# One chip core, three chained layers: coarse attention computed once per pair of units instead of once per unit

## The chip, the cores and the metric

The kernel runs on one core of a Trainium2 chip. The metric is device time in microseconds of one execution of the whole program. Three runs of the kernel before gave 643.84, 644.37 and 645.01 us (median 644.37).

## The reference

Three layers follow each other. The change touches the coarse half of the first.

```python
# first layer: B=4, H=8, S=576, D=64, factor=4, Sd=144
q_d = q.reshape(B, H, Sd, factor, D).mean(axis=3)      # k_d, v_d likewise
out_d = sm_attn(q_d, k_d, v_d)                         # softmax(q_d k_d^T / 8) v_d
out_up = np.repeat(out_d, factor, axis=2)
...
scores = np.where(|i - j| < factor, scale * q k^T, -1e9)
out_local = softmax(scores) v
attn_out = out_up + out_local
# second layer: token mixing, then channel mixing
u = x + (relu(x^T w_tok1) w_tok2)^T
x2 = u + relu(u w_ch1) w_ch2
# third layer: four causal attention experts, the two best of a gate mixed
```

## The kernel before, in words

A **unit** is one batch and one pair of heads: 16 units, numbered `4*b + p`. Head 0 of a unit lies on partitions 0 to 63, head 1 on 64 to 127. A **pair** `k` is units `2k` and `2k+1`. The first stage of the program is the attention of all units and the token mixing of each pair (`half`), woven together; the channel mixing (tiles `c`, line 219) and the third layer follow.

The order of every instruction of the first stage is written out by hand in the table `STEPS`: each word is a step and its unit, pair or part, and the words are issued from left to right, each engine taking its own instructions in that order. An instruction that waits holds everything behind it on its engine. Steps of a unit that matter here: `q` and `v` load; `qd`, `kd`, `pv` add up groups of four; `sl` is the local scores (band and product, TensorE), `mx`, `ex`, `sm`, `rs`, `P` their softmax, `tl` and `tc` turn and copy the result. The coarse attention of a unit is `sd` (scores, TensorE), `md` (maximum, VectorE), `ed` (Exp with its sum, ScalarE), `rd` (reciprocal of the sum, VectorE), `Pd` (scaling, GpSimd), `pdt` (six transposes) and `pc` (copy out of PSUM, tile `PdT`). Steps of a pair: `ol` is the product with the values for both units (coarse and local), `oc` and `ad` copy and add it into `u`. Steps of the token mixing of a pair: `tx` (turn `u`), `xh`, `xl` (split in two parts; `xr` is the rest of 64 rows), `h` (first product), `hh`, `hl`, `pu` (second product), `ua` (add into `u`). Words such as `w0`, `g0`, `t0`, `a0`, `f0`, `gd0`, `add0`, `hi0`, `lo0` load and convert the weights.

In the coarse scores of a unit the 144 pooled queries lie in two blocks of 72 (`c`) and the result stands on 72 partitions; `h` selects the half of the array's rows and the PSUM bank:

```python
for c in range(2):
    for h in range(2):
        mm(sd[:72, h, c * SD:(c + 1) * SD], qd[64 * h:64 * h + 64, c * 72:(c + 1) * 72],
           kd[64 * h:64 * h + 64, :], start=True, stop=True)
```

PSUM has four single banks (`b1`: `tl`, `pdt`, `ol`, `tx`, `h`, `pu`) and two double banks (`b2`) in this stage; `sl` and `sd` take the double ones in turn.

Of the kernel before, what the change touches and what calls it, by code (L numbers as in the profile page):

```python
# [7 lines left out]
F32 = mybir.dt.float32  # L8
# [4 lines left out]
AF = mybir.ActivationFunctionType  # L13
OP = mybir.AluOpType
# [14 lines left out]
PB = 3  # L29
# [22 lines left out]
    q0 sl0 q1 qd0 mx0 kd0 kd1 w0 g0 t0 w1 qd1 sd1 sb0 gd0 a0 ex0 sl1 f0 q2 g1 md1 sm0 mx1 ed1 gd1 rd1 q3 a1 rs0 add0  # L52
    sl2 hi0 ex1 qd2 kd2 w2 f1 t1 mx2 sd0 sb2 lo0 g2 sl3 Pd1 pdt1 md0 q4 qd4 gd2 rs1 v0 a2 P0 t2 kd3 ex2 add1 ed0 kd4
    mx3 P1 pc1 w3 rd0 sl4 f2 hi1 Pd0 ex3 tl0.0 tl0.1 sm2 tc0.0 add2 v1 tl1.0 pdt0 q5 lo1 pv0 w4 hi2 pv1 g3 tl1.1 mx4
    sd2 qd3 sb4 rs2 lo2 pc0 tc1.0 ex4 rs3 sd3 gd3 q6 md2 tc1.1 a3 tc0.1 P3 md3 t3 g4 ed2 gd4 ol0.0 a4 ol0.1 f3 f4
    kd5 oc0 ed3 sd4 ad0.0 add3 t4 ad0.3 ad0.2 ad0.1 tl3.0 md4 P2 tx0.1 rd3 hi3 add4 lo3 tc3.0 xh0.1 tx0.0 tx0.2
    tl3.1 xh0.0 v2 q7 xh0.2 ed4 Pd3 xl0.1 xl0.0 sl5 xl0.2 pdt3 pv2 tl2.0 sl6 rd2 sm4 hi4 tc3.1 w5 Pd2 kd6 mx5 tc2.0
    g5 qd5 t5 h0.0 gd5 tl2.1 rs4 v3 a5 f5 ex5 q8 h0.1 w6 lo4 mx6 sd5 pc3 tc2.1 qd6 hh0 pdt2 add5 P4 sb6 hi5 tl4.0 g6
    pc2 sd6 tc4.0 hl0 pv3 ol1.0 md5 ol1.1 t6 ed5 sl7 q9 lo5 gd6 v4 rd4 a6 md6 f6 oc1 add6 ed6 kd7 ad1.0 ad1.2 ad1.1
    pu0.0 ad1.3 mx7 tl4.1 tx1.0 rs5 tx1.1 hi6 tc4.1 xh1.0 lo6 ua0.0 v5 sl8 xh1.1 P5 rd6 Pd4 pu0.1 pu0.2 ex7 xl1.0 w7  # L60
    ua0.1 q10 pv4 xl1.1 qd7 kd9 q11 tx1.2 ua0.2 xh1.2 xl1.2 pdt4 qd9 tl5.0 rd5 sd7 pv5 h1.0 Pd5 kd10 w8 qd8 md7 ex6
    pc4 g7 Pd6 pu0.3 h1.1 mx8 sb8 kd8 sl9 v6 ed7 hh1 ua0.3 q12 sm6 tc5.0 v7 rs7 hl1 pdt5 mx9 rd7 g8 gd8 rs6 pc5
    tl5.1 pu1.0 P6 tc5.1 ua1.0 ex9 gd7 sd8 ol2.0 md8 P7 pu1.1 Pd7 oc2 ex8 ed8 pv6 ua1.1 v8 q13 sd9 pu1.2 rs9 ad2.0
# [82 lines left out]
def body(ctx, tc, qT, kT, vw, vp, wt1, wt2, wc1, wc2, wq, wk, wvg, wo, out):  # L146
# [193 lines left out]
    NR = pa.tile([72, 6], F32, name="ndraw")  # L340
    SR = [pa.tile([72, 6], F32, name=f"sdm{i}") for i in range(3)]
    for x in (NR, *SR):
        nc.gpsimd.memset(x, 1.0)

    turns = {"pd": 0, "vr": 0, "sr": 0}

    def rotate(nm, tiles):
        turns[nm] += 1
        return tiles[(turns[nm] - 1) % len(tiles)]

    def unit(i):
# [16 lines left out]
        def pool_q():  # L368
            r["qd"] = pa.tile([128, SD], F32, tag="qd", bufs=4, name="qd")
            nc.vector.tensor_reduce(r["qd"], r["q"].rearrange("p (g r) -> p g r", r=4), axis=AX.X, op=OP.add)  # L370
# [69 lines left out]
        def down():  # L440
            sd, qd, kd = b2("sd"), r["qd"], r["kd"]
            for c in range(2):
                for h in range(2):
                    mm(sd[:72, h, c * SD:(c + 1) * SD], qd[64 * h:64 * h + 64, c * 72:(c + 1) * 72],  # L444
                                     kd[64 * h:64 * h + 64, :], start=True, stop=True)
            r["sd"] = sd[:72, :, :2 * SD].rearrange("p h (c k) -> p h c k", c=2)

        def down_max():
            nd = r["nd"] = pa.tile([72, 3, 3], F32, tag="nd", bufs=3, name="nd")
            nc.vector.tensor_reduce(NR[:, :4].rearrange("p (h c) -> p h c", h=2), r["sd"], axis=AX.X, op=OP.max, negate=True)  # L450
            nc.vector.tensor_scalar_mul(nd[:, :, :2], NR.rearrange("p (h c) -> p h c", c=2), 1.0 / 128.0)

        def down_exp():
            Pd = r["Pd"] = rotate("pd", PD)
            sdm = r["sr"] = rotate("sr", SR)
            for h in range(2):
                for c in range(2):
                    nc.scalar.activation(Pd[:, :, c, h, :KD], r["sd"][:, h, c].rearrange("p (j k) -> p j k", k=KD), AF.Exp, bias=r["nd"][:, h, c:c + 1],
                                         scale=1.0 / 128.0, accum_out=sdm[:, 2 * c + h:2 * c + h + 1])

        def down_sum():
            rd = pa.tile([72, 3, 3], F32, tag="rd", bufs=3, name="rd")
            nc.vector.tensor_scalar(rd[:, :, :2], r["sr"].rearrange("p (c h) -> p c h", h=2), 1e-9, 4.0, op0=OP.add, op1=OP.mult)
            r["rd"] = pa.tile([72, 4], F32, tag="rd4", bufs=3, name="rd4")
            nc.vector.reciprocal(r["rd"].rearrange("p (c h) -> p c h", h=2), rd[:, :2, :2])

        def down_norm():
            P4 = r["Pd"].rearrange("p j c h n -> p j (c h) n")[:, :, :, :KD]
            nc.gpsimd.tensor_tensor(P4, P4, r["rd"][:, None, :, None].to_broadcast([72, 3, 4, KD]), op=OP.mult)

        def turn_down():
            pd = r["pdt"] = b1("pdt")
            for j in range(3):
                for c in range(2):
                    o = j * SD + c * 72
                    tp(pd[:, o:o + 72], r["Pd"][:, j, c].rearrange("p h n -> p (h n)"), ident[:72, :72])

        def keep_down():
            r["PdT"] = pa.tile([128, 3, SD], F32, tag="PdT", bufs=4, name="PdT")
            nc.scalar.activation(r["PdT"].rearrange("p j n -> p (j n)"), r["pdt"][:, :3 * SD], AF.Copy)  # L480
# [583 lines left out]
```

## Time and profile before

| | before |
|---|---|
| median of three runs | 644.37 us |
| profiled execution | 644.59 us, of which span 642.5 us |
| TensorE (PE) busy | 618.0 us, 96% |
| VectorE (DVE) busy | 443.6 us, 69% |
| ScalarE (ACT) busy | 361.5 us, 56% |
| GpSimd (POOL) busy | 149.5 us, 23% |

The span runs from the first to the last instruction that the profiler saw; 2.1 us of the execution lie around it. Busy shares are means over the span: the first 48 us, the rest of the first stage, the channel mixing and the third layer differ. TensorE's matmuls overlap each other, so the duration of one is longer than the distance to the next; distances are what add up.

### The profile page before, as it was taken

Reading aid. Unit: us, or ns where it says so; the run is one execution under the profiler, and the core shown is the slowest. Engines: PE = TensorE matmul, PEld = TensorE weight load, DVE = VectorE, ACT = ScalarE, POOL = GpSimd, SP = SyncE. Lnnn points to the kernel's source line nnn. Section 1 sums busy time; section 2 is a strip of 40 time slices with the busy share of each in tenths; the row PEclk is TensorE's granted clock in tenths of the full one; section 3 lists DMA queues with packets and bytes.
Section 4 is the critical chain, followed back from the end, with each engine's and each line's share of the span. In section 5 each row is a group of like instructions: output and inputs, shape, how many; then the busy total and the mean of one; then the engine's idle time right before and its main releaser. Section 6 shows DMA issues by size and latency. Waiting matters only on the chain.

```text
span 642.5 us, 13638 instructions
## 1 busy us (share of the span) xinstructions
PE 618.0 (96%) x5196; PEld 554.6 (86%) x5196; DVE 443.6 (69%) x1083; ACT 361.5 (56%) x1061; POOL 149.5 (23%) x167
## 2 busy tenths in 40 slices
PE   4789999999999999999999999999989999999997
PEld 3678889999988889998888889999989889989885
DVE  7999998779696876467644554443497766857871
ACT  4898977765464453343422332420488777777783
POOL 6878986522131120010000000310010020010000
PEclk9999999999999999999999999999999999999999
DMA  8879484013132220020200100000111121021103
GB/s 266 250 234 279 130 248 119 13 46 116 42 106 88 66 87 12 1 66 0 67 0 1 51 16 1 2 0 1 44 35 37 29 76 38 20 100 40 37 33 117
DMA packets 28945, 46.76 MB, mean 73 GB/s; under 512 B 3216, under 2 KB 16016, under 8 KB 28880
## 3 DMA queue, kind: packets, MB, share of 16 engines
q1 hardware_dynamic: 28880, 45.90, 23.8%
q8 instruction: 41, 0.67, 0.5%
q14 instruction: 24, 0.20, 0.1%
HBM read 36.45 MB, written 4.72 MB: 64 GB/s over the span
## 4 chain that ended last, share of the span: by engine, by line
PE 87%; DVE 9%; DMA 1%; issue 1%; ACT 1%; POOL 1%; SPq 0%; ACTq 0%; DVEq 0%; POOLq 0%
PE c L219 47%; PE proj L219 7%; PE vp L219 4%; PE wo L219 4%; PE pu L219 4%; PE o L962 4%; PE pt L939 3%; PE h L219 3%; PE s L900 2%; PE s L901 2%; DMA wt_raw<-in_wt_dram 1%; PE tx L556 1%; PE sd L444 1%; DVE nraw L403 1%; PE tl L486 1%
## 5 line engine op out<-in xcount | busy, mean ns | idle before, releaser
L219 PE MATMUL c<-hl,wch 128*128 128x460 f32 (+1 forms) x240 | 89.3, 372 | 0.0
L219 PE MATMUL c<-hh,wcl 128*128 128x460 f32 (+1 forms) x240 | 89.1, 371 | 0.0
L219 PE MATMUL c<-hh,wch 128*128 128x460 f32 (+1 forms) x240 | 89.1, 371 | 0.0
L219 PE MATMUL c<-ul,wch 128*128 128x460 f32 (+1 forms) x240 | 89.0, 371 | 0.0
L219 PE MATMUL c<-uh,wch 128*128 128x460 f32 (+1 forms) x240 | 89.0, 371 | 0.0
L219 PE MATMUL c<-uh,wcl 128*128 128x460 f32 (+1 forms) x240 | 88.9, 370 | 0.0
L199 ACT ACTIVATE hh<-c 128x460 fp32r<-128x460 f32 (+1 forms) x60 | 33.0, 549 | 84.9 <-PE c L219 84.6
L795 POOL TENSOR_TENSOR vlo<-u,vh 128x576 fp32r<-128x576 f32 x16 | 22.8, 1427 | 238.7 <-ACT vh L791 215.1
L208 DVE SCALAR_TENSOR_TENSOR hl<-c,hh 128x460 fp32r<-128x460 f32 (+1 forms) x60 | 38.0, 634 | 48.7 <-ACT hh L199 48.5
L281 POOL TENSOR_TENSOR wc_t<-wc_f,wc_t 128x512 int32<-128x512 int32 x24 | 32.5, 1358 | 150.7 <-ACT wc_t L270 122.3
L663 DVE TENSOR_TENSOR ul<-u,uh 128x460 fp32r<-128x460 f32 (+1 forms) x80 | 53.1, 677 | 9.7 <-ACT uh L657 9.7
L657 ACT ACTIVATE uh<-u 128x460 fp32r<-128x460 f32 (+1 forms) x80 | 45.4, 585 | 23.8 <-PE c L219 19.0
L917 ACT ACTIVATE Pc<-Pc,nm 116x116 f32<-116x116 f32 (+4 forms) x80 | 46.7, 586 | 8.7 <-DVE nm L910 6.8
L910 DVE CUSTOM_DVE_ANT_0 Pc<-s,caus 116x348 f32<-116x348 f32 (+4 forms) x80 | 40.0, 514 | 14.6 <-PE s L901 10.9
L219 PEld LDWEIGHTS c<-hh,wch 128*128 128x128 f32 x240 | 45.2, 188 | 5.2
L219 PEld LDWEIGHTS c<-hh,wcl 128*128 128x128 f32 x240 | 45.1, 188 | 5.2
L219 PEld LDWEIGHTS c<-uh,wcl 128*128 128x128 f32 x240 | 45.1, 188 | 5.1
L219 PEld LDWEIGHTS c<-uh,wch 128*128 128x128 f32 x240 | 45.1, 188 | 5.0
L219 PEld LDWEIGHTS c<-hl,wch 128*128 128x128 f32 x240 | 45.1, 188 | 4.9
L219 PEld LDWEIGHTS c<-ul,wch 128*128 128x128 f32 x240 | 45.1, 188 | 4.9
L939 PE MATMUL pt<-ident,Pc 116*116 116x116 f32 (+2 forms) x240 | 35.2, 263 | 2.9 <-DVE Pc L928 2.6
L928 DVE TENSOR_SCALAR Pc<-Pc,su,gw 116x464 f32<-116x464 f32 (+4 forms) x80 | 36.3, 478 | 0.7
(216 smaller groups left out, 1650.6 us busy)
## 6 DMA issues: line engine op xcount, KB each, us to landing
wc_raw<-in_wc_dram SPq DMA_DIRECT2D x24, 512.0 KB, 3.6
vz<-in_vw_dram SPq DMA_DIRECT2D x16, 320.0 KB, 5.3
qT<-in_qT_dram SPq DMA_DIRECT2D x16, 288.0 KB, 5.0
kT<-in_kT_dram SPq DMA_DIRECT2D x16, 288.0 KB, 5.3
vr<-in_vp_dram SPq DMA_DIRECT2D x32, 144.0 KB, 4.2
K<-K SPq DMA_DIRECT2D x64, 72.0 KB, 2.0
out_dram<-y SPq DMA_DIRECT2D x18, 256.0 KB, 2.0
wt_raw<-in_wt_dram SPq DMA_DIRECT2D x4, 288.0 KB, 3.5
```

Source lines behind the costliest of these rows:

```text
L199: nc.scalar.activation(hi, src, AF.Relu if relu else AF.Copy, **({"scale": scale} if scale else {}))
L208: nc.vector.scalar_tensor_tensor(lo, src, 0.0, h, op0=OP.max, op1=OP.subtract)
L219: mm(ps, a, c, start=first and i == 0, stop=last and i == n - 1)
L281: nc.gpsimd.tensor_tensor(t, r["f"], t, op=OP.add)
L657: nc.scalar.activation(hi, UA[:, c, blocks[k]], AF.Copy)
L663: nc.vector.tensor_tensor(lo, UA[:, c, blocks[k]], hi.bitcast(F32), op=OP.subtract)
L795: nc.gpsimd.tensor_tensor(lo, U[b][:, c], hi.bitcast(F32), op=OP.subtract)
L910: nc.vector.tensor_tensor_reduce(dst, r["s", t, e], mask, -1.0, 3.0e38, OP.add, OP.min, nm[:nq])
L917: nc.scalar.activation(P[:nq, :n], P[:nq, :n], AF.Exp, bias=r["nm", t, e][:nq], scale=-1.0, accum_out=r["su", t][:nq, e:e + 1])
L928: nc.vector.tensor_scalar(P[:nq, :n], P[:nq, :n], r["su", t][:nq, e:e + 1], BR[b]["w"][:nq, t, 2 * p + e:2 * p + e + 1], op0=OP.mult, op1= ...
L939: tp(pt[:TS[c], (c - c0) * TQ:(c - c0) * TQ + nq], P[:nq, c * TQ:c * TQ + TS[c]], ident[:nq, :nq])
L962: mm(o[64 * e:64 * e + 64, a - q0:q1 - q0], BR[b]["VV"][:TS[c], c, ec:ec + 64], PT[e][:TS[c], column(c, a):column(c, a) + q1 - a], start=( ...
```

## The change

The coarse attention becomes a step of a pair. The 288 pooled queries of two units are cut into six blocks of 48; set `s` holds blocks `2s` and `2s+1`, one on partitions 0 to 63, one on 64 to 127. A block is issued 64 queries wide (the last 16 are the next block's, or zeros that a memset writes once), so that each score matmul uses one quarter of the array: 12 matmuls of 64 x 64 with 144 columns for a pair, where two units had 8 of 64 x 72. Maximum, Exp, reciprocal and scaling then act on 128 partitions and three sets for both units at once: one maximum over 864 numbers a partition for two over 576, six Exp for eight, one scaling over 864 for two over 576. Each (j, s) block of 112 rows is turned with a permutation `perm` in place of the identity, which drops the 16 surplus queries behind the 96 useful ones, where the next block overwrites them: nine transposes of 112 columns for twelve of 72, again in two single banks, and two copies for two. The buffers `pd` are two (of 128 partitions) instead of three; the memsets of `ndraw` and `sdm` go, memsets of `qd` and three copies that build `perm` come. The whole table `STEPS` is another one.

```diff
-PB = 3
+PB = 2
+ROWS = 64 + KD
 STEPS = """
-    q0 sl0 q1 qd0 mx0 kd0 kd1 w0 g0 t0 w1 qd1 sd1 sb0 gd0 a0 ex0 sl1 f0 q2 g1 md1 sm0 mx1 ed1 gd1 rd1 q3 a1 rs0 add0
...
+    q0 sl0 qd0 q1 mx0 sl1 sb0 qd1 ex0 w0 kd0 kd1 mx1 sm0 g0 ex1 q2 t0 rs0 kd2 gd0 w1 P0 g1 sd0 a0 f0 sl2 md0 add0
...
-    PD = [pa.tile([72, 3, 2, 2, 64], F32, name=f"pd{i}") for i in range(PB)]
+    PD = [pa.tile([128, 3, 3, 2, 64], F32, name=f"pd{i}") for i in range(PB)]
+    perm = pa.tile([ROWS, ROWS], F32, name="perm")
+    for to, at, n in ((0, 0, KD), (KD, 64, KD), (2 * KD, KD, 64 - KD)):
+        nc.vector.tensor_copy(perm[:, to:to + n], ident[:ROWS, at:at + n])
+    QD = [pa.tile([128, SD + 16], F32, name=f"qd{i}") for i in range(4)]
...
+        def down():
+            sd = b2("sd")
+            for s in range(3):
+                for c in range(2):
+                    x, t = divmod(2 * s + c, 3)
+                    for h in range(2):
+                        hs = slice(64 * h, 64 * h + 64)
+                        mm(sd[64 * c:64 * c + 64, h, s * SD:(s + 1) * SD], (A, Bu)[x]["qd"][hs, KD * t:KD * t + 64],
+                           (A, Bu)[x]["kd"][hs], start=True, stop=True)
+            r["sd"] = sd[:, :, :3 * SD].rearrange("p h (s k) -> p h s k", s=3)
...
+        def down_max():
...
+            nc.vector.tensor_reduce(raw.rearrange("p (s h) -> p h s", h=2), r["sd"], axis=AX.X, op=OP.max, negate=True)
+            nc.vector.tensor_scalar_mul(nd[:, :, :2], raw.rearrange("p (s h) -> p s h", h=2), 1.0 / 128.0)
...
+            for s, h in SH:
+                nc.scalar.activation(Pd[:, :, s, h, :KD], r["sd"][:, h, s].rearrange("p (j k) -> p j k", k=KD), AF.Exp,
+                                     bias=r["nd"][:, s, h:h + 1], scale=1.0 / 128.0, accum_out=sm[:, 2 * s + h:2 * s + h + 1])
...
+        blocks_d = [(j, s) for j in range(3) for s in range(3)]
+
+        def turn_down(part):
+            pd = r["pdt", part] = b1("pdt")
+            for n, (j, s) in enumerate(blocks_d[5 * part:5 * part + 5]):
+                tp(pd[:, 2 * KD * n:2 * KD * n + ROWS], r["Pd"][:ROWS, j, s].rearrange("p h n -> p (h n)"), perm)
...
+            n0, n1 = (0, 10 * KD, 18 * KD)[part:part + 2]
+            nc.scalar.activation(r["PdT"][:, n0:n1], r["pdt", part][:, :n1 - n0], AF.Copy)
```

How the new table moves instructions is seen in two places. The first is the start of VectorE's queue, from the first pooling `qd` to the first weight conversions (`nraw` are local maxima, `P` the local scores shifted, `sm` and `rs` their sums and reciprocals, `nd` and `ndraw` the coarse maxima, `rd` the coarse reciprocals, `wt_0_g`, `wt_0_a`, `wt_0_f` the conversion of the first weight). Before:

```order
L370 TENSOR_REDUCE qd<-qT_0_137 128x144
L403 TENSOR_REDUCE nraw<-sl 128x2x5
L370 TENSOR_REDUCE qd<-qT_1_166 128x144
L412 TENSOR_TENSOR P_0_199<-sl,nraw 128x2x5x64
L278 TENSOR_SCALAR wt_0_g<-wt_0_g 128x512
L272 TENSOR_SCALAR wt_0_a<-wt_0_g 128x512
L275 SCALAR_TENSOR_TENSOR wt_0_f<-wt_0_raw,wt_0_a 128x512
L450 TENSOR_REDUCE ndraw<-sd 72x4
```

And in the change:

```order
L371 TENSOR_REDUCE qd_111<-qT_0_139 128x144
L404 TENSOR_REDUCE nraw<-sl 128x2x5
L413 TENSOR_TENSOR P_0_200<-sl,nraw 128x2x5x64
L371 TENSOR_REDUCE qd_112<-qT_1_169 128x144
L404 TENSOR_REDUCE nraw<-sl 128x2x5
L409 TENSOR_SCALAR nmx<-nraw 128x5x2
L419 TENSOR_REDUCE sm<-P_0_200 128x10
L435 TENSOR_SCALAR rs<-sm 128x5x2
L436 RECIPROCAL rs<-rs 128x5x2
L278 TENSOR_SCALAR wt_0_g<-wt_0_g 128x512
L272 TENSOR_SCALAR wt_0_a<-wt_0_g 128x512
```

The second unit's local maximum and the first unit's sum and reciprocal now stand ahead of the first weight; the first coarse maximum follows behind `wt_0_f` in both.

The second place is TensorE's queue from the last group of coarse scores ahead of the token mixing to its first product `h`. Before:

```order
L444 MATMUL sd<-kd,qd 72x144 x4
L486 MATMUL tl<-ident,P_3_441 128x128 x3
L556 MATMUL tx_649<-ident,u 128x128 x4
L556 MATMUL tx_668<-ident,u 128x128 x4
L556 MATMUL tx_673<-ident,u 64x128 x2
...
L397 MATMUL sl<-kT_1_482,qT_1_480 64x64 x20
L476 MATMUL pdt<-ident,pd_105 128x72 x6
L486 MATMUL tl<-ident,P_2_323 128x128 x3
...
L397 MATMUL sl<-kT_2_537,qT_2_535 64x64 x20
L219 MATMUL h_795<-xh,wt_0h 128x256
```

And in the change:

```order
L475 MATMUL sd<-kd,qd_113 64x144 x6
L475 MATMUL sd<-kd,qd_112 64x144 x6
L445 MATMUL tl<-ident,P_2_414 128x128 x3
L564 MATMUL tx_769<-ident,u 64x128 x2
L506 MATMUL pdt<-perm,pd_106 128x112 x5
...
L398 MATMUL sl<-kT_3_689,qT_3_687 64x64 x20
L506 MATMUL pdt<-perm,pd_106 128x112 x4
L445 MATMUL tl<-ident,P_2_414 128x128 x2
L219 MATMUL h_856<-xh,wt_0h 128x256
```

Up to its first `h` TensorE had done the local scores of seven units, 18 turns `tl`, five coarse score groups of a unit and three of the `pdt` groups; in the change it has done the local scores of eight units, 20 turns, and three coarse score groups and two `pdt` groups of a pair.

## Rows read from the trace of the kernel before

**Rows 1.** The page: span, and busy time of each engine.
```profile
span 642.5 us, 13638 instructions
PE 618.0 (96%) x5196; PEld 554.6 (86%) x5196; DVE 443.6 (69%) x1083; ACT 361.5 (56%) x1061; POOL 149.5 (23%) x167
```

**Rows 2.** Windows: stretch, length, busy us (instructions) per engine, clock, DMA share, GB/s.
```profile
0.00:10.00 10.00, 3.55 (x56) 2.50 (x60) 5.63 (x12) 2.56 (x4) 6.00 (x23) 1.00 0.80 267
10.00:38.00 28.00, 18.20 (x394) 15.47 (x390) 27.42 (x61) 24.31 (x105) 22.40 (x26) 1.00 0.78 240
38.00:48.00 10.00, 9.66 (x191) 8.44 (x195) 9.73 (x26) 9.76 (x47) 7.32 (x9) 1.00 0.86 257
48.00:430.00 382.00, 380.94 (x3063) 344.55 (x3053) 261.60 (x499) 188.82 (x489) 99.35 (x97) 1.00 0.22 66
430.00:642.50 212.50, 205.63 (x1514) 183.66 (x1512) 139.18 (x488) 136.02 (x423) 14.38 (x13) 1.00 0.16 46
```

**Rows 3.** Chain that ended last, 0 to 170 us: start, time on it, what.
```profile
51.79 0.37 DVE u L599
52.23 1.05 PE pu L219 x6
...
79.60 0.65 PE sd L444 x8
...
114.98 1.14 PE sd L444 x16
...
116.48 0.38 PE pdt L476 x6
116.86 0.33 PE tl L486 x3
```

**Rows 4.** Groups by line, 0 to 170 us: busy us, mean ns, idle before.
```profile
L458 ACT ACTIVATE pd<-sd,nd 72x144 f32<-72x144 f32 x64 | 23.4, 383 | 4.5 <-DVE nd L451 2.7 <-POOL vd L383 1.7
L469 POOL TENSOR_TENSOR pd<-pd,rd 72x576 f32<-72x576 f32 x16 | 18.7, 1170 | 6.9 <-ACT PdT L480 3.0 <-ACT P L429 2.1 <-DVE rd L465 1.6
L458 ACT ACTIVATION_READ_ACCUMULATOR pd<-sd,nd 72x1 f32 x64 | 13.4, 210 | 0.0
L403 DVE TENSOR_REDUCE nraw<-sl 128x10 f32<-128x640 f32 x16 | 13.0, 813 | 1.5 <-PE sl L397 1.5
L450 DVE TENSOR_REDUCE ndraw<-sd 72x4 f32<-72x576 f32 x16 | 11.9, 746 | 0.5 <-PE sd L444 0.5
L465 DVE RECIPROCAL rd<-rd 72x4 f32<-72x4 f32 x16 | 2.8, 174 | 0.9
L451 DVE TENSOR_SCALAR nd<-ndraw 72x6 f32<-72x6 f32 x16 | 2.5, 155 | 0.5
L463 DVE TENSOR_SCALAR rd<-sdm 72x6 f32<-72x6 f32 x16 | 2.4, 148 | 0.3 <-ACT pd L458 0.2
```

**Rows 5.** VectorE in order of time: start, us, what [idle before <-releaser].
```profile
5.85 0.83 DVE L403 TENSOR_REDUCE nraw<-sl 128x10 f32<-128x640 f32 x1 [1.48 <-PE sl L397]
...
9.42 0.43 DVE L278 TENSOR_SCALAR wt_g<-wt_g 128x512 f32<-128x512 f32 x1 [1.35 <-ACT wt_g L268]
...
38.16 0.42 DVE L212 TENSOR_TENSOR xr<-tx,xr 64x256 fp32r<-64x256 f32 x1
```

**Rows 6.** GpSimd in order of time: the second unit's keys.
```profile
7.44 0.67 POOL L376 TENSOR_TENSOR pool<-kT 128x288 f32<-128x288 f32 x1 [1.55 <-DMA kT<-in_kT_dram]
```

**Rows 7.** TensorE in order of time, to the first product h.
```profile
10.10 1.28 PE L397 MATMUL sl<-kT,qT 64*64 64x64 f32 x40
...
29.80 0.33 PE L522 MATMUL olx<-PdT,vd 48*64 48x144 f32 x1
...
30.58 0.21 PE L531 MATMUL olx<-PT,vz 64*64 64x58 f32 x1
...
36.87 0.75 PE L397 MATMUL sl<-kT,qT 64*64 64x64 f32 x40
...
39.69 0.39 PE L219 MATMUL h<-xh,wt_0h 128*128 128x256 f32 x1
```

**Rows 8.** Waits of TensorE, 0 to 170 us: total us, times, longest.
```profile
PE sl L390 <- ACT pd L458: 3.5, 2, 2.2
```

More of the change, by code (lines that the diff above doesn't have):

```diff
@@ new lines @@
+    a8 pu2.3 ex12 h3.1 lo7 oc4 md6 rd5 qd14 f8 ed6 ua2.3 rs10 ad4.0 ad4.1 t8 hh3 add8 hl3 sl14 ol4.1 mx14 ad4.3
+    ad4.2 pu3.0 pu3.1 ua3.0 g9 hi8 tx4.2 tl11.0 xh4.2 w10 sb14 ua3.1 tx4.0 xl4.2 kd15 xh4.0 tc11.0 tx4.1 Pd5 v11
+    tl11.1 xh4.1 P10 xl4.0 gd9 rd6 xl4.1 sd7 tc11.1 sl13 tl10.0 pdt5.0 tl10.1 lo8 pv11 pdt5.1 sm12 t9 md7 tc10.0
+    pc5.0 pu3.2 pc5.1 g10 ex14 tc10.1 h4.0 a9 pu3.3 h4.1 v12 f9 mx13 ua3.2 sm14 gd10 rs12 ed7 ol5.0 hh4 add9 sl15
+    ua3.3 hl4 oc5 ol5.1 ad5.0 ad5.1 pu4.0 P12 ex13 mx15 ad5.3 pv12 pu4.1 ad5.2 ua4.0 tx5.2 rd7 xh5.2 Pd6 ua4.1 tx5.1
@@ new lines @@
+    uh0.3 tx7.1 a11 tx7.0 lo10 t11 h6.0 ul0.1 h6.1 w12 ul0.3 hh6 xh7.2 g12 ul0.2 ul0.0 xl7.2 fc0.0 t12 xh7.0 xh7.1
+    hl6 gd12 gh0.0 gl0.0 fc0.1 f11 add11 hi11 a12 fc0.2 xl7.1 xl7.0 uh1.2 lo11 f12 pu6.0 gh0.1 h7.0 uh1.3 add12
+    pu6.1 h7.1 pu6.2 gh0.2 uh1.1 uh1.0 ul1.0 gl0.2 gl0.1 hi12 ua6.1 ua6.0 lo12 sc0.1 uh2.2 ul2.2 ul1.2 ua6.2 sc0.0
+    ul1.1 ul1.3 pu6.3 ac0.1 hh7 ac0.0 fc1.0 hl7 gh1.0 pu7.0 gl1.0 sc0.2 ac0.2 fc1.1 pu7.1 fc1.2 gh1.1 ua7.0 gl1.1
+    uh2.1 pu7.2 sc0.3 ua6.3 ua7.1 pu7.3 gh1.2 uh2.0 ul2.1 gl1.2 ul2.0 uh2.3 ul2.3 ac0.3 ua7.2 ua7.3
@@ L332, in tok_weight @@
         return convert_f64(wt2[m * 128:(m + 1) * 128, s * HS:(s + 1) * HS], [128, HS], f"wt2_{m}{s}", second)
-    PD = [pa.tile([72, 3, 2, 2, 64], F32, name=f"pd{i}") for i in range(PB)]
+    PD = [pa.tile([128, 3, 3, 2, 64], F32, name=f"pd{i}") for i in range(PB)]
[3 more added lines that the diff above has]
+    QD = [pa.tile([128, SD + 16], F32, name=f"qd{i}") for i in range(4)]
     VR = [pa.tile([128, 3, 4, D], F32, name=f"vr{i}") for i in range(RB)]
+    for x in QD:
+        nc.vector.memset(x[:, SD:], 0.0)
     for x in PD:
-        nc.vector.memset(x[:, :, :, :, KD:].rearrange("p j c h n -> p (j c h) n"), 0.0)
+        nc.vector.memset(x[:, :, :, :, KD:].rearrange("p j s h n -> p (j s h) n"), 0.0)
     for x in VR:
         nc.vector.memset(x.rearrange("p j r d -> p (j r d)"), 0.0)
[L340 to L345, printed above, removed]
+    turns = {"pd": 0, "vr": 0, "qd": 0}
     def rotate(nm, tiles):
@@ L368, in pool_q @@
         def pool_q():
[L369 to L370 removed]
+            r["qd"] = rotate("qd", QD)
+            nc.vector.tensor_reduce(r["qd"][:, :SD], r["q"].rearrange("p (g r) -> p g r", r=4), axis=AX.X, op=OP.add)
         def pool_k():
@@ L438, in local_norm @@
             nc.gpsimd.tensor_tensor(r["P"], r["P"], r["rs"][:, :, :, None].to_broadcast([128, NT, 2, WIN]), op=OP.mult)
[L440 to L480, printed above, removed]
         def turn(part):
@@ L495, in unit @@
                      sm=local_total,
-                     rs=local_sum, P=local_norm, sd=down, md=down_max, ed=down_exp, rd=down_sum, Pd=down_norm, pdt=turn_down,
-                     pc=keep_down, tl=turn, tc=keep)
+                     rs=local_sum, P=local_norm, tl=turn, tc=keep)
         return steps, r
@@ L506, in pair @@
         r = {}
+        SH = [(s, h) for s in range(3) for h in range(2)]
+        def down():
[8 more added lines that the diff above has]
+            r["sd"] = sd[:, :, :3 * SD].rearrange("p h (s k) -> p h s k", s=3)
@@ new lines, in down_sum, with down_norm @@
+        def down_sum():
+            rd = pa.tile([128, 3, 3], F32, tag="rd", bufs=2, name="rd")
+            nc.vector.tensor_scalar(rd[:, :, :2], r["dm"].rearrange("p (s h) -> p s h", h=2), 1e-9, 4.0, op0=OP.add, op1=OP.mult)
+            r["rd"] = pa.tile([128, 6], F32, tag="rd6", bufs=2, name="rd6")
+            nc.vector.reciprocal(r["rd"].rearrange("p (s h) -> p s h", h=2), rd[:, :, :2])
+        def down_norm():
+            P4 = r["Pd"].rearrange("p j s h n -> p j (s h) n")[:, :, :, :KD]
+            nc.gpsimd.tensor_tensor(P4, P4, r["rd"][:, None, :, None].to_broadcast([128, 3, 6, KD]), op=OP.mult)
@@ new lines, in pair, with keep_down @@
+        blocks_d = [(j, s) for j in range(3) for s in range(3)]
[3 more added lines that the diff above has]
+                tp(pd[:, 2 * KD * n:2 * KD * n + ROWS], r["Pd"][:ROWS, j, s].rearrange("p h n -> p (h n)"), perm)
+        def keep_down(part):
+            if part == 0:
+                T = pa.tile([128, 3, 2, SD], F32, tag="PdT", bufs=2, name="PdT")
+                A["PdT"], Bu["PdT"], r["PdT"] = T[:, :, 0], T[:, :, 1], T.rearrange("p j u n -> p (j u n)")
+            n0, n1 = (0, 10 * KD, 18 * KD)[part:part + 2]
+            nc.scalar.activation(r["PdT"][:, n0:n1], r["pdt", part][:, :n1 - n0], AF.Copy)
```

60 lines of the change are left out of this document (27 added, 33 removed).

## The prediction

> **What bounds the kernel now.** I read the windows first [rows 2]. The reader is to see where TensorE stands still: 6.5 us of the first 10, 9.8 of the next 28, 0.3 of the next 10, then 1.1 in 382 us, and 6.9 in the third layer, which the change does not touch. So from about 40 us to 430 us TensorE has no room, and time is saved there only by giving it less to do. Before that VectorE leads: it is busy 27.42 of 28 us between 10 and 38 us, while its first 10 us hold 4.4 us of idle time. The chain of work says the same from the other end [rows 3]: it runs over VectorE up to 52.16 us and over TensorE from there. The page [rows 1] shows no other engine near its limit over the span, though ScalarE and GpSimd are both over 80% busy from 10 to 38 us.
>
> That gives a way to count. Take one point at which TensorE becomes the bound, the first product `h` of the token mixing, at 39.69 us [rows 7]. The end of the span is then the time of that point, plus TensorE's work behind it, plus what TensorE waits behind it (1.4 us up to 430 us now: 0.34 in the third and 1.06 in the fourth row of [rows 2]). The change acts on each of the three.
>
> **The change part by part. TensorE's work.** A unit's coarse scores take 0.65 us of TensorE as one group and 1.14 us as two in a row [rows 3], so 0.57 to 0.65; I take 0.61. The new group, 12 matmuls of 64 x 64 and 144 columns for a pair, does not occur as scores, but the coarse half of `ol` is 12 matmuls of 48 x 64 with 144 columns, whose four quarters work side by side: from 29.80 to 30.58 us, 0.78 us [rows 7]. Above it the bound is no overlap between the two column halves: 12 matmuls at the old pace (0.61 / 4 = 0.15 each) make 1.83 us. The nearest row has the same quarters, the same columns and the same instruction, so I take 0.78. A pair then costs 0.78 for 1.22.
>
> A turn of a unit is six transposes of 72 columns in 0.38 us; a `tl` group of three with 128 columns takes 0.33, 0.11 each [rows 3]. Cost goes with the columns, so one of 112 columns takes 0.096 and nine take 0.87, for 0.76 before: 0.11 more per pair. If a transpose had a floor instead (0.063, the 72-column price) it would be 0.57, a gain of 0.19; the `tl` row speaks against it.
>
> Behind the first `h` there are now 11 score groups and 13 turns left, 11 x 0.61 + 13 x 0.38 = 11.65 us; in the change 5 pairs' scores and 6 pairs' turns, 5 x 0.78 + 6 x 0.87 = 9.1 us. That is 2.5 us less. The table also puts one more unit's local scores and two more `tl` ahead of the first `h` (eight units and 20, for seven and 18): 0.75 [rows 7] and 0.22, another 1.0 us that no longer stands behind. Sum: 3.5 us less work behind the point.
>
> **When the first h comes.** Ahead of it stands VectorE's queue up to `xr`, which begins at 38.16 us [rows 5]. From that queue go three of five coarse maxima. One over 576 numbers takes 0.746, the local one over 640 takes 0.813 [rows 4], 1.05 ns a number, so one over 864 comes to 1.05 us; that the new ones fill 128 partitions for 72 adds nothing by the same pair of rows, since the local one has 128. Five of 0.746 against two of 1.05 are 1.6 us, three `nd` of 0.155 are 0.5, one denominator (0.148 and 0.174) is 0.3: 2.4 us less. To it come two more local maxima (1.6), one pooling over 576 numbers (0.75 by the `ndraw` row), one shift and one sum over 640 (0.8 each by the `nraw` row), and about a dozen small instructions (one `nmx`, one `rs` pair, one weight step, the copies for `perm`, memsets), 1.5 us together at 0.15 or less for each: 5.5 us more. Net 3.1 us more queue.
>
> Against that, idle time at the start goes. Now VectorE waits 1.35 us for the first weight at 9.42 us [rows 5]; in the change the second unit's maximum, the first unit's sum and reciprocal stand in that gap, over 1.7 us of work. A new wait is bounded by the second unit's keys, which land at 7.44 us [rows 6]: its scores then take until 8.72 at the early pace of 1.28 us [rows 7], and VectorE, which today is through with the same two poolings, maximum and shift at 8.07 (9.42 less 1.35), waits 0.65 us. Net 0.7 us less idle. So `xr` moves from 38.16 to about 40.6, a little less since neighbouring VectorE instructions overlap by some hundredths each. But `h` began 1.53 us after `xr` began, behind a score group of TensorE's own; its first 12 products need only `xl`, which ends as `xr` begins. In the change no such group of TensorE's work has to be late: I put the first `h` between 39.2 and 41.0, and take 40.0, 0.3 us later than now.
>
> **The other engines.** ScalarE does six Exp for eight at unchanged size: two times 23.4 / 64 = 0.37 us [rows 4] less per pair, 5.8 us in all; the copies move 864 columns as before. GpSimd's scaling is one of 864 numbers for two of 576 at 1170 ns: by size 1.76 us for 2.34, 4.6 us in all. VectorE loses 2 x 1.22 us of coarse work a pair (the four means of [rows 4]) and gets 1.05 + 0.155 + 0.148 + 0.174 = 1.53 back, 7.4 us in all less 0.7 of setup. These three I cost at nothing on the path behind 40 us, since TensorE's work covers them now [rows 2]; if that cover failed they would be worth something to the change, never against it.
>
> [...] The row of TensorE's waits shows a local score group standing twice behind the Exp of a coarse group, 3.5 us in total, the longest 2.2 [rows 8]: the two double banks were both held. With 9.8 us idle before 38 us this costs nothing by itself. [...]
>
> **Sum.** -3.5 + 0.3 = -3.2 us, with waits behind the point left at 1.4 us. The profiled span of 642.5 becomes 639.3, the profiled execution of 644.59 becomes 641.4; it lies 0.2 above the median, so I predict 641.2 us.
>
> **The rivals.** *The front shortens too* (15%): ScalarE's and GpSimd's smaller load brings the first values earlier, and the first `h` comes at 38.0, since the products `h` need `xr` last and the queue's overlap takes off more than I allow. 2.0 us less than the sum: 639.2. For it: both engines are over 80% busy there [rows 2]. Against: VectorE is fuller still.
>
> *The scores do not go in quarters* (18%, with the other ways in which the gain is swallowed): column halves that write one bank take turns, 1.83 us a pair; behind the first `h` that is 5 x 1.05 = 5.2 us more than I counted, and the result 646 would follow; overlap of half of it gives 643.8, which is where I put the case. Against it: the `ol` row has just these halves in one bank.
>
> *The banks are held longer* (12%), the case that ends slower. A pair's scores hold a double bank for one maximum (1.05), one `nd` and six Exp (6 x 0.37): 3.4 us, for 2.4 in a unit now, 1.0 us more, in a pool of two; `sl` of the next unit and everything behind it in TensorE's queue waits. Now this costs nothing after 40 us because another bank was free in time. Two groups that expose their 1.0 us bring the sum within 0.2% of now, five make it slower by more than that, all eight give 649; the case is centred on 646. Against it: only half as many groups take the bank.
>
> **How the numbers follow.** The forecast, 641.2, has a chance of 55%, with a range of its own of 639.9 to 642.9 (first `h` from 39.2 to 41.0, score groups within 0.1, one more microsecond of waits in a new order). The rivals stand at 639.2 (15%), 643.8 (18%) and 646 (12%). The range that holds 8 in 10 reaches from 638.8 to 644.9. Two runs of one kernel differ by about 0.2%, 1.3 us, which is what a measurement can tell: faster means below 643.1. Forecast and first rival lie there almost whole, with a small part of the second: 70%. Within 0.2% falls most of the second and a little of its neighbours: 18%. Slower: 12%.
>
> **What would show it.** In the changed trace a group of 12 score matmuls (24 records) advances TensorE by 0.75 to 0.85 us, nine transposes by 0.85 to 0.9; a coarse maximum takes 1.05 us, six Exp 2.2 us, the scaling 1.75 us. VectorE's wait ahead of the first weight is gone and the second unit's maximum begins near 8.7 us. The first `h` begins at 40.0, within 1 us, and the first channel product about 3 us earlier than now. It is wrong if `sl` waits for the coarse Exp behind 40 us, if the first `h` slips past 43 us, or if TensorE's idle time between 48 and 430 us grows beyond 3 us.

## The result, and the profile after

| | before | after |
|---|---|---|
| median | 644.81 us (6 runs, 643.84 to 645.94) | 649.12 us (6 runs, 647.3 to 651.29) |
| ratio, 95% interval | | 1.0062 [1.0038, 1.0085] |
| profiled execution, span | 644.59, 642.5 us | 651.29, 649.5 us |

The change makes the kernel 0.6% slower; forecast was 0.5% faster. The execution profiled is the slowest of the six, so its span is 7.0 us longer, where the medians differ by 4.3. The page and the windows of the changed kernel, to be held against [rows 1, 2]:

```profile
span 649.5 us, 13631 instructions
PE 619.3 (95%) x5236; PEld 557.6 (86%) x5236; DVE 438.8 (68%) x1057; ACT 356.4 (55%) x1029; POOL 142.5 (22%) x155
```

```profile
0.00:10.00 10.00, 4.68 (x108) 3.88 (x112) 6.42 (x18) 2.69 (x3) 5.87 (x19) 1.00 0.79 272
10.00:38.00 28.00, 14.57 (x376) 12.08 (x371) 24.51 (x55) 23.20 (x107) 20.97 (x23) 0.99 0.78 237
38.00:48.00 10.00, 10.00 (x119) 8.88 (x119) 5.98 (x13) 5.67 (x17) 3.79 (x5) 0.70 0.56 189
48.00:430.00 382.00, 377.44 (x3107) 342.55 (x3106) 260.15 (x481) 188.17 (x481) 97.51 (x96) 1.00 0.23 68
430.00:649.50 219.50, 212.62 (x1540) 190.22 (x1539) 141.76 (x493) 136.69 (x423) 14.35 (x13) 0.99 0.16 44
```

TensorE's page row says nothing: its busy time even rose by 1.3 us. The windows do. Between 10 and 38 us it worked 3.6 us less than before, and VectorE, which was to be full there, 2.9 us less: from 38 to 48 us VectorE is busy 6.0 us of 10, where it had 9.7. Something stopped both. In the third row the clock column reads 0.70, and that row's 10.00 busy microseconds hold 119 matmuls, where [rows 2] shows 191 in 9.66. The chain that ended last names the place:

```profile
32.53 0.06 PE sl L391
32.59 0.51 PE sl L398 x32
33.10 4.79 issue
37.89 0.48 PE sl L398 x4
38.37 0.83 PE tl L445 x3
...
41.34 1.65 PE sd L475 x24
```

In the middle of one unit's local scores, behind the first value product (`ol`), TensorE stands still for 4.79 us, and the releaser is "issue": no semaphore that the profile shows, so nothing in the program that it waits for. Behind it the work is slow: three `tl` took 0.33 us before [rows 3] and take 0.83 now. The granted clock in stretches of 2 us (columns as in [rows 2]) shows that as well:

```profile
26.00:28.00 2.00, 2.00 (x34) 1.57 (x30) 1.97 (x5) 1.95 (x5) 1.77 (x4) 1.00 1.04 335
28.00:30.00 2.00, 1.03 (x46) 0.76 (x42) 1.97 (x5) 1.92 (x8) 1.92 (x3) 1.00 1.00 347
30.00:32.00 2.00, 1.62 (x84) 1.62 (x87) 1.93 (x6) 2.00 (x11) 1.92 (x4) 1.00 1.04 296
32.00:34.00 2.00, 1.10 (x71) 1.00 (x64) 2.00 (x6) 2.00 (x13) 1.73 (x3) 1.00 0.98 224
34.00:36.00 2.00, 0.00 (x0) 0.00 (x0) 1.49 (x6) 1.63 (x12) 0.66 (x1) 1.00 0.71 163
36.00:38.00 2.00, 0.11 (x4) 0.11 (x5) 0.00 (x0) 0.00 (x0) 1.02 (x1) 0.80 0.06 13
38.00:40.00 2.00, 2.00 (x14) 1.88 (x14) 0.83 (x1) 0.00 (x0) 0.00 (x0) 0.50 0.04 8
...
42.00:44.00 2.00, 2.00 (x25) 1.54 (x18) 0.97 (x4) 0.18 (x1) 1.92 (x4) 0.50 0.74 205
44.00:46.00 2.00, 2.00 (x56) 1.79 (x55) 0.94 (x3) 1.77 (x5) 1.15 (x1) 0.99 1.03 362
```

The engine did nothing from 33.1 to 37.9 us, the clock fell to 0.50 in that time, at about 37.2 (0.80 over 36 to 38), and stayed there until about 44. DMA was full (0.98 to 1.04) from 26 us to the stop. What came in shortly ahead of the stop's end is in the DMA view of the stretch 34.9 to 36.5 us (queue, kind: packets, MB, share), which the stretches 28 to 33 and 33 to 34.9 us lack:

```profile
q8 instruction: 1, 0.02, 5.0%
```

One transfer of 16,384 B on an instruction queue; its record starts at 35.03 us and takes 1.28, and TensorE goes on 1.58 us after its end. That the queue is TensorE's is the author's reading of a count: q8 made 41 such transfers in the execution, and the page has 10,472 matmuls and weight loads, 255 for each.

First `h` in TensorE's order of time, and the first two places on VectorE that the prediction spoke of ([rows 5] before):

```profile
46.03 0.36 PE L219 MATMUL h<-xh,wt_0h 128*128 128x256 f32 x1
```

```profile
9.13 0.82 DVE L404 TENSOR_REDUCE nraw<-sl 128x10 f32<-128x640 f32 x1 [0.99 <-PE sl L398]
...
11.24 0.36 DVE L278 TENSOR_SCALAR wt_g<-wt_g 128x512 f32<-128x512 f32 x1
```

The prices of the new operations (groups, 0 to 170 us):

```profile
L488 ACT ACTIVATE pd<-sd,nd 128x144 f32<-128x144 f32 x48 | 17.5, 387 | 4.2 <-DVE rd L493 2.2 <-DVE nd L483 1.9
L499 POOL TENSOR_TENSOR pd<-pd,rd 128x864 f32<-128x864 f32 x8 | 13.6, 1704 | 3.3 <-DVE rd L495 3.3
L482 DVE TENSOR_REDUCE draw<-sd 128x6 f32<-128x864 f32 x8 | 8.4, 1052 | 1.6 <-PE sd L475 1.6
```

### The profile page after: what moved, and what is told of

It is laid out like the page before. It is cut to its first block, busy times and chain, and to the rows that moved or that the text cites. A ratio compares the mean times of both kernels' runs of the same rounds, so it can differ in the third digit from the quotient of the medians.

```text
span 649.5 us, 13631 instructions
## 1 busy us (share of the span) xinstructions
PE 619.3 (95%) x5236; PEld 557.6 (86%) x5236; DVE 438.8 (68%) x1057; ACT 356.4 (55%) x1029; POOL 142.5 (22%) x155
## 4 chain that ended last, share of the span: by engine, by line
PE 82%; DVE 9%; POOL 2%; ACT 2%; issue 2%; DMA 2%; SPq 0%; POOLq 0%; ACTq 0%; DVEq 0%
PE c L219 46%; PE proj L219 7%; PE vp L219 4%; PE wo L219 4%; PE o L970 4%; PE pt L947 3%; PE s L908 2%; PE s L909 2%; PE pu L219 2%; PE h L219 2%; PE tx L564 1%; ACT pd L488 1%; DMA kT<-in_kT_dram 1%; DVE draw L482 1%; PE tl L445 1%
## 5 line engine op out<-in xcount | busy, mean ns | idle before, releaser
L700 DVE TENSOR_TENSOR acc<-c,acc 128x460 f32<-128x460 f32 (+1 forms) x40 | 25.4, 636 | 17.0 <-PE c L219 16.0
```

Of the source, the lines that this page charges most:

```text
L700: nc.vector.tensor_tensor(dst[:, c, sl], cs_["s", g, k, c][:, :NB[k]], src[:, c, sl], op=OP.add)
```

## The experiments

**Theories.** *Theory 1*: TensorE ran out of instructions. Its stream is taken to come in blocks of 256, by the 255 of that count; the block that begins in these local scores was asked for when the one before it began (an assumption of the author's: no trace shows when a block is asked for), lay behind the loads, and came late, because the dense value product and what follows used up 256 instructions in 2.4 us. *Theory 2*: the coupled step itself costs, through banks held longer and coarse results that come later (the prediction's rival of the banks held longer). All padding below is work whose result nobody uses: small transposes into a PSUM slot that is not read, two instructions each (a weight load and a matmul).

**The change again** (`c1_after_again`).

> The changed kernel once more, for its time beside the others on the same chip and for a second trace. Theory 1 (TensorE ran out of fetched instructions: its next block of 256 was asked for at about 30.6 us, lay behind the weight and input loads, and came at 36.3) expects the stop behind the first value product again, 3 to 6 us long, with no semaphore behind it. If that stop was an accident of one execution, it is missing here and the time is below 647. Theory 2 (the coupled step itself costs, through longer held banks and later coarse results) does not speak of the stop. Time 647 to 651 us by both.

Measured 1.0053 [1.0033, 1.0073]. The stop in its trace:

```profile
36.34 0.49 PE L398 MATMUL sl<-kT,qT 64*64 64x64 f32 x6 [2.98 <-issue]
```

Same place, the same number of matmuls left (6), another length: the transfer started at 33.52 us here. It is no accident of one execution, and its length varies from one to the next (4.79 and 2.98 us).

**40 transposes at the head** (`e4_pad40`).

```diff
     with tc.manual_schedule():
+        pad = b1("pad")
+        for _ in range(40):
+            tp(pad[:32, :32], ident[:32, :32], ident[:32, :32])
         for n in steps[:cut]:
```

> The changed kernel with 40 transposes of 32 x 32 at the head of TensorE's queue, which nobody reads; they run while the first loads are on their way and move every block of 256 instructions by 80 against the work. Theory 1: the end of a block no longer falls behind the value product, the next block is asked for earlier against the work, and the stop shrinks by 2 us or more: 644.5 to 647. Theory 2, and a theory in which the order of the work makes the wait: the stop and the time stay, 648.5 to 650.

Measured 0.9983 [0.9968, 0.9998]: 644.6 us, 4.3 less than the changed kernel beside it (648.93), and a little faster than before. TensorE in order of time, where the stop was, and then the windows of this run:

```profile
32.87 0.55 PE L445 MATMUL tl<-ident,P 128*128 128x128 f32 x3
33.76 0.88 PE L564 MATMUL tx<-ident,u 128*128 128x128 f32 x4 [0.34 <-DVE u L547]
...
35.50 0.97 PE L475 MATMUL sd<-kd,qd 64*64 64x144 f32 x24 [0.20 <-ACT P L430]
...
39.14 0.38 PE L219 MATMUL h<-xh,wt_0h 128*128 128x256 f32 x1
```

```profile
38.00:48.00 10.00, 8.31 (x221) 7.56 (x213) 9.67 (x20) 8.11 (x34) 6.54 (x9) 1.00 0.95 280
48.00:430.00 382.00, 379.78 (x2996) 344.88 (x2987) 257.84 (x475) 183.33 (x458) 93.63 (x91) 1.00 0.21 65
```

No stop, clock 1.00, first `h` at 39.14 us; the program behind the transposes is the changed kernel's.

**128 transposes** (`e5_pad128`): which tells theory 1 from any good that padding does by itself.

```diff
+        pads(40)
         for n in steps[:cut]:
+            if n == ("sl", 2, None):
+                pads(44)
+            if n == ("sl", 4, None):
+                pads(44)
```

> The changed kernel with 128 of the small transposes that nobody reads: 40 at the head and 44 each ahead of the local scores of the third and the fifth unit, where TensorE waits 2.8 us anyway. They are 256 instructions, one whole block: the ends of blocks fall on the same work again as without them. Theory 1 (a late block of instructions): the stop behind the first value product comes back, 2 to 5 us long, time 646.5 to 651. If the 40 of the run before helped by something else (TensorE kept busy early, another turn of the PSUM buffers), 128 help as well: no stop, 643.5 to 645.5.

Measured 1.0050 [1.0032, 1.0068]; the stop is back in TensorE's order of time:

```profile
36.43 0.34 PE L398 MATMUL sl<-kT,qT 64*64 64x64 f32 x6 [2.83 <-issue]
```

Counted from 0 in the trace's list of TensorE's records (waits for semaphores among them), the first instruction behind the stop is number 961 in the changed kernel in both traces, and 1217 here: 256 more, at the same work. Record 705, with which by this count the block before begins, came at 30.69 us in the changed kernel, so its 256 records were used up in 2.4 us; in the kernel before, records 705 to 961 took 7.9 us (31.23 to 39.13).

**The same 40 in the kernel before** (`e4b_before_pad40`).

> The kernel before with the same 40 transposes at its head. It had no stop without a semaphore of over 0.2 us ahead of 48 us, so theory 1 has nothing to take away: 644.5 to 646.5, or slower where the moved blocks now end at a dense place. If the transposes help in themselves (by a busier TensorE early), it gets faster by 1 us or more.

Measured 1.0033 [1.0020, 1.0046]: what frees the one kernel harms the other, by 1.9 us (648.37 for 646.45). A stop appears in TensorE's order of time that was not there, again without a semaphore, at record 1473 = 961 + 2 x 256:

```profile
49.91 0.47 PE L397 MATMUL sl<-kT,qT 64*64 64x64 f32 x17 [1.14 <-issue]
```

A second one, of 0.66 us, stands at 111.9 us; together they are 1.8 us.

**Fewer loads on the way** (`e6_values_later`).

```diff
-    ... lo3 v2 kd4 rd1 tl3.1 tx0.0 v3 sd2 ... mx6 w6 add4 ...
+    ... lo3 kd4 rd1 tl3.1 tx0.0 sd2 ... mx6 w6 v2 v3 add4 ...
```

> The changed kernel with the value loads of the third and fourth unit taken behind the seventh weight's load, which is issued at 39.9 us: the instructions of TensorE stand as in the changed kernel, but from about 34.5 us no load is on its way. Theory 1 in the form that the block lay behind the loads: it starts at 31 to 33 us instead of 33.5 and 35.0, and the stop is at most 1.5 us. If the fetch takes its time whatever the loads do, the stop stays at 3 to 5 us. The values are then late for the second value product, 2 to 4 us of a wait near 46 us that is new, so the time says little: 645 to 650.

Measured 1.0053 [1.0034, 1.0072]. TensorE's order is the changed kernel's, the stop is at the same record 961, but the transfer starts at 31.07 us in place of 33.52 and 35.03, and the stop is short:

```profile
33.82 0.34 PE L398 MATMUL sl<-kT,qT 64*64 64x64 f32 x6 [1.06 <-issue]
```

First `h` came at 39.1 us. The transfer began 4.3 us behind record 705 in the changed kernel, 2.6 in `c1` and 0.7 here, where the loads' queue q1 has a share of 0.9% from 30.5 to 32.5 us (101.1% from 28 to 33 us in the changed kernel). That speaks for a block that lay behind the loads, and about 1 us of stop is left without them. The values were late as expected (waits of 3.5 and 1.1 us behind the first `h`), which took the gain back.

**The local scores moved** (`e3_sl6_after_tx`).

```diff
-    ... ad0.3 a4 sl6 tl3.0 kd5 tx0.1 ... tl3.1 tx0.0 v3 sd2 ... xl0.1 tx0.2 sb6 ...
+    ... ad0.3 a4 tl3.0 kd5 tx0.1 ... tl3.1 tx0.0 v3 tx0.2 sl6 sd2 ... xl0.1 sb6 ...
```

> The changed kernel with the seventh unit's local scores moved from directly behind the first value product to behind the first three turns tx, so that fewer instructions are ready when the next block is late. Theory 1: TensorE still stops, but for work that it has to wait for anyway: first h 1 to 4 us earlier than 46.0, time 645 to 648. Theory 2: no change, 648.5 to 650.

Measured 1.0018 [1.0004, 1.0032], first `h` at 42.6 us. The word `tx0.2` moved as well, to stand ahead of `sl6`. In the local scores no stop without a semaphore is left (TensorE's waits from 36 us on list one of 1.2 us, at a `tx`): the block's transfer ended at 34.65 us, and record 961 came only at 37.42, since TensorE waited for other engines on the way, longest ahead of this instruction:

```profile
36.69 0.41 PE L564 MATMUL tx<-ident,u 128*64 128x128 f32 x2 [0.97 <-ACT PT L451]
```

The time falls by as much as theory 1 said; that TensorE would still stop for that block, as it said too, does not show.

**The coupled code under the old table** (`e1_new_code_old_table`): each coarse word of a pair once, where the second unit's word stood.

> The coupled coarse step under the old table, each pair's word where the second unit's word stood (one qd buffer less and one kd buffer more, since units are held otherwise). Theory 1: the work behind the first value product is spread as in the kernel before, TensorE does not run dry there, and the smaller work shows: first h within 1 us of 39.7, time 640.5 to 643. Theory 2: the loss comes along with the code: 647 or more.

Measured 1.0062 [1.0041, 1.0083], first `h` at 41.5 us. Both numbers of theory 1 are missed, and the time is that of theory 2. But a stop without a semaphore is not what makes the loss: behind the first value product stands a wait with a semaphore, and the clock falls behind it too (0.86 from 38 to 48 us); TensorE in order of time:

```profile
34.70 0.87 PE L445 MATMUL tl<-ident,P 128*128 128x128 f32 x3 [2.75 <-DVE u L547]
```

The turn waits for the sums of that product into `u`, by the program for a PSUM bank. The run leaves open whether the coupled step costs this by itself, as theory 2 has it, or because the old order does not suit it.

**What is left, and the best version.** With the stop gone, the waits of the new order show. `e7_pad40_pv3` (and once more `e7b_again`) is the run with 40 and one word moved:

```diff
-    ... pc1.1 t5 qd7 ... hi5 tl4.0 pv3 gd6 ol1.0 ...
+    ... pc1.1 pv3 t5 qd7 ... hi5 tl4.0 gd6 ol1.0 ...
```

> The changed kernel with the 40 transposes at the head, and with the pooling of the fourth unit's values put ahead of a weight conversion that GpSimd waited 1.8 us for. The second value product waited 1.4 us for these values. If that wait is one of those that the new table leaves behind, it goes and the time falls by 1 to 1.5 us against the run with 40 alone: 643.0 to 644.0. If another is late next, no change: 644.6.

> The last variant (40 transposes at the head, the fourth unit's values pooled earlier) once more, as the measure for the three beside it. Its trace showed the wait for the values replaced by one of 1.3 us for the bank of the product h, and the channel products no earlier than with 40 transposes alone; its smaller time was then only the third layer's clock. If that is so, its time lies between 643.4 and 645, at 0.996 to 0.999 of the kernel before.

Measured 0.9958 [0.9943, 0.9974] and 0.9967 [0.9954, 0.9979]. In the first trace the last channel product ends no earlier than with 40 alone (447.3 us in both), in the second 0.8 us earlier. The longest wait of TensorE from 36 to 60 us, in `e4`:

```profile
PE oly L529 <- POOL vd L384: 1.4, 1, 1.4
```

and in `e7b`, in the same value product:

```profile
PE olx L538 <- DVE h1l L208: 1.3, 1, 1.3
```

One took the place of the other, so the smaller ratios are not explained by the wait that the word was to remove.

`e8_pad20_pv3` and `e9_pad60_pv3` replace the 40 by 20 and 60:

> The same with 20 transposes in place of 40: the end of the block falls 40 instructions later against the work, into the first of the local scores behind the value product, and the block is asked for near 29 us, when TensorE comes to the value product. Theory 1: a stop of 0 to 2 us there, between none (with 40) and 3 to 4.8 us (without); first h later by about as much, time 0 to 2 us above the run with 40. If only the number of early transposes counts and not where the block ends, no stop and the same time.

> The same with 60: the end of the block falls 40 instructions earlier than with 40, into the value product itself, and the block before it is asked for by 27.5 us. Theory 1: no stop, or under 1 us, time within 1 us of the run with 40, but for stops that now appear where another block ends at a dense place.

Measured 0.9981 [0.9968, 0.9994] and 0.9962 [0.9949, 0.9975], neither with a stop near 33 us (with 60 there is one of 0.7 us at 50.9, "issue" again). With 20 the block's transfer was over at 31.3 us, in time. Of the five amounts 0 and 128 stop there, 20, 40 and 60 do not.

`e10_two_more`:

```diff
-    ... gd6 ol1.0 t6 kd7 rs5 hl0 a6 ... f7 ol2.0 ua1.0 sb8 rd3 ...
+    ... hl0 gd6 ol1.0 t6 kd7 rs5 a6 ... sb8 f7 ol2.0 ua1.0 rd3 ...
```

> The variant with 40 with two more words moved on VectorE's queue: the rest of the first product h (which frees its bank) ahead of a weight conversion, and one unit's shift ahead of another conversion and a sum into u. They aim at the two waits left that the table makes: 1.3 us of the second value product for the bank and 1.1 us of the fifth pair's scores for a bank. If these waits cost what they show, channel products come 1.5 to 2.3 us earlier: 641.5 to 643. If others take their place, no change against the run with 40.

Measured 0.9962 [0.9949, 0.9975]: no change. One wait of the two is gone, the other fell from 1.3 to 1.0 us, and the channel products end 0.2 us earlier, not 1.5: small waits of `tx`, `tl` and `pu` are next.

`e11_three_slots` spreads the 40 over three slots; `e12_third_filled` adds 70 transposes in the third layer, ahead of the first turn `pt`; `e14_again` repeats that one, beside the kernel before with the same filling (`e13_before_filled`):

```diff
+        for count in (38, 1, 1):
+            pads(count)
...
             pt = r["pt", g, e] = b1("pt")
+            if not filled:
+                filled.append(1)
+                for _ in range(70):
+                    tp(pt[:32, :32], ident[:32, :32], ident[:32, :32])
```

> The best variant so far (40 transposes at the head, three words moved) with its transposes spread over three slots of the single banks instead of one. With one slot the first value projection of the third layer waited 0.73 us for a sum into u, which the kernel before and the run with three slots (128 transposes) did not. If the turn of the banks makes that wait, it goes, and the projections end 2.8 to 3.4 us earlier than in the kernel before instead of 2.2: time 642.0 to 643.0, 0.7 to 1.2 us below the variant with one slot. If not, the wait is there again and the time stays at 643.5.

> The same with 70 more transposes that nobody reads, issued in the third layer ahead of the first turn of its probabilities, where TensorE stands still for 2.5 us in every kernel here. They put nothing on the path unless they last longer than the stand. If the 1.35 us that the changed kernel loses behind it are the granted clock, it stays at 1.00 between 470 and 490 us, and the time falls by 1.2 to 1.4 us against the run beside it where that one shows the drop. If something else is late there, the time stays.

> The kernel before with the 70 transposes in the third layer's stand and nothing else. Its profiled execution did not show the drop of the clock behind the stand, but its runs spread over 3 us. If the drop comes in part of its executions too, the filling takes 0.5 to 1.3 us off its median: 0.998 to 0.9992 of the kernel before. If the drop belongs to the new order alone, no change.

> The variant with the transposes at the head in three slots, three words moved and the third layer's stand filled, beside it on the same chip. Against the kernel before with the same filling it is what the coupled step is worth without the stop: by the traces 2.1 to 2.7 us at the end of the channel mixing, so 0.9935 to 0.9955 of the kernel before, and 2 to 3 us below the run beside it.

Measured: 0.9953 [0.9939, 0.9967] with three slots, 0.9942 [0.9927, 0.9957] and 0.9935 [0.9922, 0.9949] with the filling, 0.9990 [0.9980, 0.9999] for the kernel before with it. Three slots took the wait of the first value projection away, as expected. The windows of that variant:

```profile
38.00:48.00 10.00, 9.01 (x232) 8.26 (x231) 9.67 (x22) 8.72 (x38) 7.23 (x9) 1.00 0.99 282
48.00:430.00 382.00, 380.14 (x2982) 344.75 (x2982) 257.61 (x475) 182.91 (x455) 93.08 (x91) 1.00 0.22 65
430.00:639.80 209.80, 202.90 (x1501) 181.12 (x1499) 137.99 (x486) 135.68 (x422) 14.38 (x13) 1.00 0.16 46
```

The third layer stays open. The changed kernel loses 1.4 us there, where the clock reads 0.83 in one stretch of 10 us (480 to 490) behind a stand of 2.6 us, and the kernel before has a stand of 2.6 us in its profiled execution without that drop. With the stand filled, `e12`'s trace shows 1.00 throughout. But the kernel before with the same filling does drop, as does the repeat (first row of `e13`, second of `e14`):

```profile
476.00:478.00 2.00, 2.00 (x11) 1.92 (x10) 1.83 (x5) 1.70 (x7) 0.92 (x2) 0.50 0.00 0
```

```profile
474.00:476.00 2.00, 2.00 (x12) 1.92 (x10) 1.40 (x3) 1.66 (x6) 0.79 (x2) 0.50 0.00 0
```

In `e4b`, the kernel before with transposes at the head alone, the clock drops there too. The record has the mean granted clock of each execution: that profiled one of the kernel before reads 0.999, and of the 23 executions of this kernel beside `c1` only six read that, the other 17 read 0.991 to 0.997. The drop, 0.50 for 3.4 us in the changed kernel's trace, is worth 0.003 of this mean by an estimate (half of 3.4 in 642.5 us), so most executions of the kernel before lost clock somewhere that the profiled one did not; where, no trace shows. So the drop meets variants of both kernels, filled or not, and nothing here ties it to the change. What decides it was not found, nor why the filled kernels are a little faster in the median.

## Why the prediction was wrong

**The first h: the step that failed.** The prediction put it at 40.0 us by VectorE's queue alone, between 39.2 and 41.0; it came at 46.03. Not VectorE was late: its first weight was at 11.24 us, the early wait had gone (one of 0.99 us, forecast 0.65, came in its place), and with the blocks shifted the first `h` stood at 39.14 us (`e4`), 0.9 earlier than forecast. There `xr` began at 38.67 us, not at about 40.6: the longer queue of VectorE was priced too high by 1.9 us, for a reason that was not worked out. What the sum lacked, by these runs, is TensorE's own supply of instructions. The new table puts the seventh unit's local scores directly behind the value product: 256 instructions that were ready to go in 2.4 us, while the loads kept DMA full (0.98 to 1.04). In the kernel before the blocks end elsewhere against the work; moved by 80 instructions, they stop it too (`e4b`, 1.14 and 0.66 us). What the traces show of that supply is the size (16,384 B on q8 for 255 instructions), stops 256 records apart (961, 1217, 1473), and in `e6` a transfer that began 2.5 and 4.0 us earlier with fewer loads on the way. When a block is asked for was not shown and stays an assumption.

**What the stop dragged along.** First `h` came 6.3 us later than before (46.03 for 39.69), or 6.9 later than without the stop (39.14): 4.8 are the stop, and 2.2 the slower work behind it: from the instruction of the stop to the first `h` TensorE's work, idle time left out, took 8.1 us here, 7.1 in `c1` and 5.9 in `e4`, with the clock at 0.50 for 6.8, 3.4 and 0 us. In `c1` a stop of 2.98 us put the first `h` at 44.3.

**TensorE's work behind the point: right.** Forecast 3.5 us less. Summing how far each group moves TensorE's end on, idle time left out, from the first `h` to the last channel product, in the kernel before and in `e11`: scores 7.05 and 4.24 us (forecast 6.7 and 3.9), turns `pdt` 5.61 and 5.35 (forecast 0.28 more, not 0.26 less), local scores 7.04 and 6.29 (forecast 0.75 less), turns `tl` 7.77 and 8.01 (forecast 0.22 less, not 0.24 more), everything together 4.1 us less (3.9 in the changed kernel itself). The groups with a forecast make 3.6 of it; the rest are groups whose number of instructions did not change. The scores do go in quarters, 0.85 us a pair, so that rival falls; the maximum took 1.05 us, six Exp 2.2 and the scaling 1.70, as forecast (1.05, 2.2, 1.75).

**The waits behind: a smaller miss.** Forecast unchanged at 1.4 us. In the changed kernel TensorE is idle 4.56 us from 48 to 430, and the 3.2 us more outweigh most of the gain in work. The longest waits are:

```profile
PE tx L564 <- DVE xr L212: 1.1, 1, 1.1
PE sd L475 <- DVE rd L493: 1.1, 1, 1.1
PE sd L475 <- POOL kd L378: 0.8, 1, 0.8
```

With the stop gone they are 3.9 us behind the first `h` (`e4`) and 2.85 (`e11`). They are queues in an order that does not fit, one behind the other (`e7`, `e10`); none is the rival of `sl` behind the coarse Exp, which does not occur behind 40 us. That rival's sign came true without its mechanism. So without the stop the gain would still have fallen short: `e4`, the changed kernel with nothing but padding, lies 0.8 us below the kernel before beside it (644.6 and 645.39), not 3.2.

**The sum.** 6.3 us more at the first `h`, 3.9 less work, 3.2 more waits and 1.4 in the third layer make 7.0, by which the profiled span grew. One variant does reach the size of the forecast: `e14`, with its padding and three moved words, stands 3.1 us below the kernel before with the same filling (641.64 and 644.74 us). That is partly luck, since the terms do not agree: in the trace of `e11`, the same variant unfilled, the first `h` comes 0.1 us earlier than before (forecast 0.3 later), the work is 4.1 less (3.5) and the waits are 1.45 more (none), 2.7 us less at the end of the channel mixing.

## What to carry to other kernels

Where the releaser of an idle engine is "issue", as in the 4.79 us here, the profile shows nothing in the program that it waits for: look at the instruction queues in the DMA view beside it (here q8, one transfer of 16,384 B), and at whether it has just run through a few hundred small instructions while loads fill DMA (here 256 in 2.4 us, at 0.98 to 1.04). When a change makes a stretch denser, count the instructions that become ready together, not only their time. A few dummy instructions at the head, with a whole block of them as the control, told such a stop here from a cost of the work or its order, and are worth trying before a change is judged.

## What the runs showed of the hardware

TensorE stood still without a semaphore for 4.79, 2.98, 2.83, 1.06 and 1.14 us in five runs (the changed kernel, `c1`, `e5`, `e6`, `e4b`). In the changed kernel, `c1` and `e6` it went on 1.4 to 1.6 us after the end of a 16,384 B transfer on queue q8. The place of the stop moved with the number of instructions ahead: from record 961 to 1217 with 256 more (`e5`). Instructions added at the head cost or saved microseconds far behind: 40 transposes, 80 instructions, took 4.3 us from one kernel (`e4`) and put 1.9 us onto another (`e4b`).
